# Holding back the first stores of a fused attention and channel-mix kernel, and moving its norms

## The chip, the cores and the metric

The kernel runs on one core of one Trainium2 chip. The metric is the device time of one execution in microseconds. Most executions of a kernel lie close together, but some are slower; a run more than 1.5% above the fastest of its kernel is called slow. Ratios are computed as the mean time of one kernel's fast runs over that of the other's fast runs of the same rounds, so they are not quite the ratio of the medians quoted beside them; the brackets are 95% intervals. A median is that of all runs, slow ones included; where that matters, the fast runs are named. The experiments ran on different chips (numbers 8, 11, 7, 15 and 2), so ratios compare kernels within one only.

## The reference

Two parts: cross-covariance attention over channels (256 x 256 per batch, 4 batches, 6208 rows), then an RWKV channel mix of the result.

```python
def _attn_ref(q, k, v, tau):
    qn = q / (np.linalg.norm(q, axis=1, keepdims=True) + 1e-06)
    kn = k / (np.linalg.norm(k, axis=1, keepdims=True) + 1e-06)
    s = kn.transpose(0, 2, 1) @ qn / tau
    s = s - s.max(-1, keepdims=True)
    a = np.exp(s)
    a /= a.sum(-1, keepdims=True) + 1e-09
    return (v @ a).astype(np.float32)

def _moe_ref(x, mu_k, mu_r, w_k, w_v, w_r):      # x_prev: x shifted by one row
    xk = mu_k * x + (1.0 - mu_k) * x_prev
    xr = mu_r * x + (1.0 - mu_r) * x_prev
    k = np.maximum(xk @ w_k, 0.0)
    v = k * k @ w_v
    r = 1.0 / (1.0 + np.exp(-(xr @ w_r)))
    return (r * v).astype(np.float32)
```

## The kernel before

After batch 0's q and k have been loaded and its softmax is done, the kernel walks through 48 blocks of 512 rows and a short last one. In the steps of block i it also multiplies q and k of the next batch (the "units"), loads v of block i + 6, transposes v of block i + 5 with a DMA, and computes x of block i + 2. SyncE issues both the v transposes and the stores of the results, in the order of the program (its ten issues from 64.13 to 118.33 us stand in that order in the profile of before):

```python
# in the steps of block i
if j == 0 and 4 <= i + 6 < NBLK - 1:
    v_load(i + 6)                    # GpSimd queue, 6 tiles
...
if j == 5 and 4 <= i + 5 < NBLK - 1:
    v_transpose(i + 5)               # SyncE queue, 5 tiles

def finish(i, s):                    # a quarter of block i's result; the last one in step 1 of block i + 1
    nc.scalar.activation(res[:, s], vr_ps[:, D:], AF.Tanh, scale=0.5)
    nc.vector.scalar_tensor_tensor(res[:, s], res[:, s], 1.0, vr_ps[:, :D], op0=OP.add, op1=OP.mult)
    ...
    if i < NBLK - 2:
        if s == S - 1:
            nc.sync.dma_start(dst, res)      # 512 KB, SyncE queue, res has 3 tiles
```

The sums of squares of batch 1 to 3 are added on VectorE; when the last add has been issued, the piece `norms` (four matmuls with one column, line L279) may be issued in the very next step:

```python
if len(chain) == NORMS and any(e[1] == holds[0] for e in adds):
    piece = None                     # norms wait for the last add
else:
    chain.pop(0)
```

Of the kernel before, what the change touches and what calls it, by code (L numbers as in the profile page):

```python
# [18 lines left out]
def kernel(  # L19
# [58 lines left out]
    bank = {}  # L78
    st_ps = {}
    adds = []  # L80
    sums = {}
    now = [0]
    groups = {}
# [29 lines left out]
    def group_load(b, g):  # L113
        rows, n = rows_of(b, g)
        if b == 0:
            t_f = []
            for i, t in enumerate((q, k)):
                f = pq.tile([P, S, C], F32, name=f"f{i}", tag=f"f{i}", bufs=6)
                (nc.sync if g else nc.scalar).dma_start(f[:rows, :n], qk_src(t, b, g))  # L119
                t_f.append(f)  # L120
            groups[b, g] = tuple(t_f)
        else:
            qk = pq.tile([P, S, 2, C], BF16, name="qk", tag="qk", bufs=5)
            groups[b, g] = (qk,)
            for i, t in enumerate((q, k)):
                nc.gpsimd.dma_start(rows_at(qk, b, g, i)[:rows, :n], qk_src(t, b, g))  # L126
# [79 lines left out]
    def unit_square(b, g, s):  # L206

        rows, n = rows_of(b, g)
        if s % 2:
            return  # L210
        qk = groups[b, g][0]
        if n == 1:
            t = sums[b, "left"] = pq.tile([P, 1, 2 * C], BF16, name="sq", tag="sq1", bufs=2)
            nc.scalar.activation(t[:rows], qk[:rows].rearrange("p s i c -> p s (i c)")[:, :1], AF.Square)
            return
        if s == 0:
            sums[b, g] = pq.tile([P, S, 2 * C], BF16, name="sq4", tag=f"f{g % 2}", bufs=6)
        t = sums[b, g]
        to = t[:, s:s + 2].rearrange("p s (i c) -> p i s c", i=2)
        if apart(b, g):  # L220
            nc.scalar.activation(to, qk.rearrange("p s i c -> p (s i c)").rearrange(
                "p (i s c) -> p i s c", i=2, s=S)[:, :, s:s + 2], AF.Square)
        else:
            nc.scalar.activation(t[:, s:s + 2], qk[:, s:s + 2].rearrange("p s i c -> p s (i c)"), AF.Square)  # L224
        if s == 2:
            adds.append((now[0] + 2, b, lambda: pairs_add(b, g)))
            adds.append((now[0] + 3, b, lambda: quad_add(b, g)))
# [38 lines left out]
    def softmax_pieces(b):  # L266

        s_ps = cov.pop(b) if b else None
        rn = pn.tile([P, 4], F32, name="rn")
        s_sb = pn.tile([P, 2, C], F32, name="s_sb")  # L270
        e_sb = pn.tile([P, 2, C], F32, name="e_sb", bufs=1)
        mx = pn.tile([P, 2], F32, name="mx")
        sm = pn.tile([P, 2], F32, name="sm")
        rk = rn[:, 2:4]
        def norms():
            bank[b] = ps.tile([P, 4], F32, name="bank", tag="xT_ps", bufs=2)
            t = sums.pop(b)
            for i in range(4):
                nc.tensor.matmul(bank[b][:, i:i + 1], t[:, i * P:(i + 1) * P], ones[:, 0:1],  # L279
                                 start=i == 0, stop=True, skip_group_check=True)  # L280

        def roots():
            nc.scalar.copy(rn, bank[b])

        def diagonals():
            dg = pn.tile([P, 2, P], F32, name="dg", tag="dg", bufs=1)
            for h in range(2):
                nc.vector.tensor_tensor(dg[:, h], cov[0][h][:, 3 * P * h:3 * P * h + P], ident_f, op=OP.mult)
            nc.vector.tensor_reduce(rn[:, 0:2], dg, axis=AX, op=OP.add)

        def root(h):
            nc.scalar.activation(rn[:, 2 * h:2 * h + 2], bank[0][:, 0:2] if h else rn[:, 0:2], AF.Sqrt)

        def invert_first(h):
            nc.vector.tensor_scalar_add(rn[:, 2 * h:2 * h + 2], rn[:, 2 * h:2 * h + 2], 1e-6)
            nc.vector.reciprocal(rn[:, 2 * h:2 * h + 2], rn[:, 2 * h:2 * h + 2])
            if h and inv_tau != 1.0:
                nc.vector.tensor_scalar_mul(rk, rk, inv_tau)

        def evac_first():  # L300
            for h in range(2):
                nc.vector.tensor_scalar_mul(s_sb[:, h], cov[0][h][:, P:P + C], rn[:, h:h + 1])

        def pow2():
            nc.gpsimd.tensor_tensor(rn, rn, half, op=OP.pow)

        def invert():
            nc.vector.tensor_scalar_add(rn, rn, 1e-6)
            nc.vector.reciprocal(rn, rn)
            for h in range(2):  # L310
                nc.vector.tensor_scalar_mul(s_sb[:, h], s_sb[:, h], rn[:, h:h + 1])
            if inv_tau != 1.0:
                nc.vector.tensor_scalar_mul(rk, rk, inv_tau)

        def evac():
            nc.scalar.copy(s_sb, s_ps)

        def turn():

            st_ps[b] = ps.tile([P, 2, C], F32, name="st_ps", tag="xT_ps", bufs=2)  # L320
            for n in range(4):
                ih, dh = divmod(n, 2) if b else (n % 2, n // 2)
                nc.tensor.transpose(st_ps[b][:, ih, dh * P:(dh + 1) * P], s_sb[:, dh, ih * P:(ih + 1) * P],  # L323
                                    ident_f)

        def exp(halves=range(2)):
            for ih in halves:
                if not bounded:
                    nc.vector.tensor_reduce(mx[:, ih:ih + 1], st_ps[b][:, ih], axis=AX, op=OP.max, negate=True)
                    nc.vector.tensor_tensor(mx[:, ih:ih + 1], mx[:, ih:ih + 1], rk[:, ih:ih + 1], op=OP.mult)  # L330
                nc.scalar.activation(e_sb[:, ih], st_ps[b][:, ih], AF.Exp, scale=rk[:, ih:ih + 1],
                                     bias=0.0 if bounded else mx[:, ih:ih + 1],
                                     accum_out=sm[:, ih:ih + 1])

        def shares():
            nc.vector.reciprocal(sm, sm)

        def weigh(ih):
            nc.scalar.activation(a_sb[:, b, ih, :], e_sb[:, ih], AF.Copy, scale=sm[:, ih:ih + 1])

        def weigh_first(ih):
            nc.vector.reciprocal(sm[:, ih:ih + 1], sm[:, ih:ih + 1])
            nc.vector.tensor_scalar_mul(a_sb[:, b, ih, :], e_sb[:, ih], sm[:, ih:ih + 1])

        if b == 0:
            return diagonals, root, invert_first, evac_first, turn, exp, weigh_first

        return [evac, None, norms, roots, pow2, None, invert, None, None, turn, lambda: exp([0]), lambda: exp([1]),
                shares, lambda: weigh(0), lambda: weigh(1)]

    blocks = [(b, t) for b in range(B) for t in range(NB)] + ["left"]
    NBLK = len(blocks)
    L1 = L + 1
    xl = const.tile([P, 2, B, L1], BF16, name="xl")
    st = {}

# [35 lines left out]

    def x_half(i, dh):
        b, t = blocks[i]
        if dh == 0:
            xT = p2.tile([P, 2, M + 1], BF16, name="xT", tag="xT", bufs=3)
            st[i, "x"] = xT
            if t == 0:
                nc.vector.memset(xT[:, :, 0:1], 0.0)
            else:  # L400
                nc.scalar.copy(xT[:, :, 0:1], st[i - 1, "x"][:, :, M:M + 1])
        xT = st[i, "x"]
        vT = st[i, "vT"]
        xT_ps = ps.tile([P, M], F32, name="xT_ps", tag="xT_ps", bufs=2)
        for ih in range(2):
            nc.tensor.matmul(xT_ps, a_sb[:, b, ih, dh * P:(dh + 1) * P], vT[:, :, ih, :],  # L406
                             start=ih == 0, stop=ih == 1)
        nc.scalar.copy(xT[:, dh, 1:], xT_ps)  # L408
# [120 lines left out]
    def down(i, j):  # L529
# [3 lines left out]
            return  # L533
        kk = st[i, "kk"]
        if j == 0:
            st[i, "res"] = p2.tile([P, S, D], F32, name="res", tag="res", bufs=3)
        if h == 0:
            vr_ps = ps.tile([P, 2 * D], F32, name="vr_ps", tag="vr_ps", bufs=2)
            st[i, "vr"] = vr_ps
# [9 lines left out]
    def finish(i, s):  # L549
# [8 lines left out]
        dst = out[b, t * M:(t + 1) * M, :].rearrange("(s p) c -> p s c", p=P)  # L558
        if i < NBLK - 2:
            if s == S - 1:  # L560
                nc.sync.dma_start(dst, res)
        elif s % 2:

            nc.sync.dma_start(dst[:, s - 1:s + 1], res[:, s - 1:s + 1])
# [1 line left out]
    def last_block(i):  # L566
# [1 line left out]
        down(i - 1, 7)  # L568
        kk, xr = st[i, "kk"], st[i, "xr"]
        SL = B * L // P  # L570
        res = p2.tile([P, S, D], F32, name="res", tag="res", bufs=3)
        r_ps = ps.tile([P, SL, D], F32, name="r_ps", tag="s_ps")
        y_ps = [ps.tile([P, D], F32, name="y_ps", tag="xT_ps", bufs=2) for _ in range(SL)]
        for s in range(SL):
# [71 lines left out]
    chain = []  # L646
    NORMS = 13
    holds = [0]

    def unit(ahead=2):  # L650

# [57 lines left out]
    for i in range(-2, NBLK - 1):  # L709
        for j in range(8):  # L710
# [6 lines left out]
                v_load(i + 6)  # L717
            if chain:
                piece = chain[0]
                if len(chain) == NORMS and any(e[1] == holds[0] for e in adds):  # L720
                    piece = None
                else:
                    chain.pop(0)
# [53 lines left out]
                unit()  # L777
            if adds and adds[0][0] <= now[0] and (j in (1, 6, 7) or adds[0][1] == holds[0] and chain):
                next_add()
            now[0] += 1  # L780
            if i >= 0 and i % NB == 2 and j == 1 and i // NB < B:
                left_go[0] = left_x(i // NB)
# [40 lines left out]
```

## Time and profile before

| | before |
|---|---|
| timed runs | 506.85, 506.85, 508.45 us |
| profiled execution | 515.58 us, span 513.8 us, slow |
| instructions | 9206 |

The top of the page (busy us, share of the span, count) and, from its fourth part, the chain that ended last by engine:

```profile
PE 480.6 (94%) x3370; PEld 330.9 (64%) x3429; DVE 431.4 (84%) x788; ACT 428.6 (83%) x869; POOL 96.4 (19%) x143
...
PE 73%; DMA 21%; DVE 2%; issue 1%; POOL 1%; ACT 1%; SPq 0%; POOLq 0%; DVEq 0%
```

PE is busy nearly always, yet a fifth of the chain is DMA: there is a stretch in which PE runs behind transfers.

### The profile page before, as it was taken

The numbers are of one execution on the slowest core, as the hardware profiler recorded it, in microseconds if no ns is written. First come the engines' busy times: TensorE is split into PE (matmuls) and PEld (weight loads), VectorE is DVE, ScalarE is ACT, GpSimd is POOL, SyncE is SP. The second block draws the span as 40 slices with busy tenths as digits, with TensorE's granted clock in tenths as the row PEclk, the third lists the DMA queues.
The fourth block names the chain that finished last, engine by engine and source line by source line (L and its number), as shares of the span: only waits on it lengthen the run. The fifth ranks groups of instructions, "written<-read, shape, count | busy, mean of one in ns | idle before, by whom it ended". The sixth has DMA issues, their size and how long they took to land.

```text
span 513.8 us, 9206 instructions
## 1 busy us (share of the span) xinstructions
PE 480.6 (94%) x3370; PEld 330.9 (64%) x3429; DVE 431.4 (84%) x788; ACT 428.6 (83%) x869; POOL 96.4 (19%) x143
## 2 busy tenths in 40 slices
PE   3579999797899999999999999999999999999996
PEld 1345677555676677677676667667666666666675
DVE  3778799957979989989988988989988787878884
ACT  5769997877889989898899989898888888878884
POOL 0043331222143132221143132200031100000000
PEclk9999999989999999999999999999999999999999
DMA  8999999999999999999799999974299673523123
GB/s 325 409 307 197 191 165 134 173 145 209 164 213 174 211 172 179 179 160 168 113 158 149 221 161 188 181 134 111 63 150 161 102 146 83 106 74 93 41 84 103
DMA packets 132694, 83.46 MB, mean 162 GB/s; under 512 B 50660, under 2 KB 125736, under 8 KB 132648
## 3 DMA queue, kind: packets, MB, share of 16 engines
q0 software_dynamic: 55824, 33.01, 50.4%
q1 hardware_dynamic: 76504, 49.59, 43.5%
q8 instruction: 27, 0.44, 0.4%
q10 hardware_dynamic: 320, 0.26, 0.2%
q14 instruction: 19, 0.16, 0.1%
HBM read 78.71 MB, written 25.43 MB: 203 GB/s over the span
## 4 chain that ended last, share of the span: by engine, by line
PE 73%; DMA 21%; DVE 2%; issue 1%; POOL 1%; ACT 1%; SPq 0%; POOLq 0%; DVEq 0%
PE vr_ps L546 28%; PE kT_ps L514 25%; DMA vT<-v_bf 11%; PE vr_ps L542 8%; PE xT_ps L406 7%; DMA f<-in_q_dram 5%; PE s_ps L263 4%; DMA v_bf<-in_v_dram 2%; DMA qk<-in_q_dram 2%; DMA qk<-in_k_dram 1%; POOL v_bf L363 0%; DVE kk L527 0%; SPq L119 0%; PE y_ps L584 0%; PE st_ps L323 0%
## 5 line engine op out<-in xcount | busy, mean ns | idle before, releaser
L519 ACT ACTIVATE kr<-kT_ps 128x512 bf16<-128x512 f32 (+1 forms) x390 | 235.0, 605 | 34.2 <-PE kT_ps L514 28.6
L546 PE MATMUL vr_ps<-w_v_sb,kk 128*128 128x256 bf16 x1536 | 230.6, 273 | 0.4
L514 PE MATMUL kT_ps<-xk,w_k_sb 128*128 128x512 bf16 (+1 forms) x722 | 218.1, 377 | 0.3 <-DVE xk L499 0.2
L546 PEld LDWEIGHTS <-kk 128*128 128x128 bf16 x1536 | 150.4, 98 | 57.5
L556 DVE SCALAR_TENSOR_TENSOR res<-res,vr_ps 128x256 f32<-128x256 f32 x192 | 80.0, 417 | 59.9 <-ACT res L555 59.9
L527 DVE TENSOR_TENSOR kk<-kr 128x2048 bf16<-128x2048 bf16 (+1 forms) x148 | 125.8, 851 | 0.2 <-ACT kr L519 0.2
L514 PEld LDWEIGHTS <-w_k_sb 128*128 128x128 bf16 x780 | 75.7, 98 | 28.0 <-issue 1.4
L555 ACT ACTIVATE res<-vr_ps 128x256 f32<-128x256 f32 x192 | 76.8, 400 | 2.3 <-PE vr_ps L546 1.3
L408 ACT CAST xT<-xT_ps 128x512 bf16<-128x512 f32 x94 | 55.9, 594 | 26.8 <-PE xT_ps L406 26.4
L542 PE MATMUL vr_ps<-w_r_sb,xr 128*128 128x256 bf16 x384 | 73.5, 273 | 2.7
L499 DVE SCALAR_TENSOR_TENSOR xk<-delta,mu_t,xT 128x512 bf16<-128x512 bf16 x94 | 70.1, 746 | 0.0
L499 DVE SCALAR_TENSOR_TENSOR xr<-delta,mu_t,xT 128x512 bf16<-128x512 bf16 x94 | 70.0, 746 | 0.0
L542 PEld LDWEIGHTS <-xr 128*128 128x128 bf16 x384 | 37.7, 98 | 45.3 <-issue 1.5
L406 PE MATMUL xT_ps<-vT,a_sb 128*128 128x512 bf16 x188 | 56.3, 381 | 6.2 <-DMA vT<-v_bf 6.2
L263 PE MATMUL s_ps<-qk 128*128 128x256 bf16 (+1 forms) x294 | 56.0, 273 | 0.0
L126 POOL DMA_DIRECT2D qk<-in_q_dram x39 | 26.1, 670 | 152.7 <-ACT kr L519 128.8
L224 ACT ACTIVATE sq<-qk 128x1024 bf16<-128x1024 bf16 x48 | 51.1, 1064 | 0.0
L363 POOL DMA_DIRECT2D v_bf<-in_v_dram x48 | 36.6, 765 | 56.3 <-DMA vT<-v_bf 35.2
L189 PE MATMUL s_ps<-qk 128*128 128x384 bf16 (+2 forms) x98 | 19.2, 339 | 17.1 <-ACT qk L146 15.2
L489 DVE TENSOR_TENSOR delta<-xT 128x1024 bf16<-128x1024 bf16 x47 | 32.2, 686 | 1.1 <-ACT xT L408 1.1
L263 PEld LDWEIGHTS <-qk 128*128 128x128 bf16 (+1 forms) x294 | 28.6, 98 | 5.7 <-issue 0.8
L126 POOL DMA_DIRECT2D qk<-in_k_dram x39 | 25.8, 662 | 19.8 <-DMA v_bf<-in_v_dram 11.2
(106 smaller groups left out, 249.8 us busy)
## 6 DMA issues: line engine op xcount, KB each, us to landing
out_dram<-res SPq DMA_DIRECT2D x47, 512.0 KB, 5.0
v_bf<-in_v_dram POOLq DMA_DIRECT2D x48, 256.0 KB, 8.1
qk<-in_q_dram POOLq DMA_DIRECT2D x36, 256.0 KB, 7.2
qk<-in_k_dram POOLq DMA_DIRECT2D x36, 256.0 KB, 8.9
f<-in_q_dram SPq DMA_DIRECT2D x11, 512.0 KB, 9.5
f<-in_k_dram SPq DMA_DIRECT2D x11, 512.0 KB, 10.0
vT<-v_bf SPq DMA_TRANSPOSE x44, 7.8
f<-in_q_dram SPq DMA_DIRECT2D x2, 256.0 KB, 9.0
```

The lines of the kernel that those rows point to most:

```text
L126: nc.gpsimd.dma_start(rows_at(qk, b, g, i)[:rows, :n], qk_src(t, b, g))
L263: nc.tensor.matmul(s_ps[:, ih, :], rows_at(qk, b, g, 0)[:rows, s, ih * P:(ih + 1) * P], rows_at(qk, b, g, 1)[:rows, s, :], start=t0 and ih ...
L406: nc.tensor.matmul(xT_ps, a_sb[:, b, ih, dh * P:(dh + 1) * P], vT[:, :, ih, :], start=ih == 0, stop=ih == 1)
L408: nc.scalar.copy(xT[:, dh, 1:], xT_ps)
L499: nc.vector.scalar_tensor_tensor(o[:, dh], st[i, "d"][:, dh], mu[:, dh:dh + 1], st[i, "x"][:, dh, :M], op0=OP.mult, op1=OP.add)
L514: nc.tensor.matmul(kT_ps[:, :m], w_k_sb[:, dh, fh * P:(fh + 1) * P], xk[:, dh, :m], start=dh == 0, stop=dh == 1)
L519: nc.scalar.activation(kr, kT_ps[:, :m], AF.Relu, scale=0.5 ** 0.5)
L527: nc.vector.tensor_tensor(st[i, "kk"][:, fh // 4 * 4 + lo:fh + 1, :m], kr, kr, op=OP.mult)
L542: nc.tensor.matmul(vr_ps[:, D:], xr[:, dh, s * P:(s + 1) * P], w_r_sb[:, dh, :], start=dh == 0, stop=dh == 1)
L546: nc.tensor.matmul(vr_ps[:, :D], kk[:, fh, s * P:(s + 1) * P], w_v_sb[:, fh, :], start=fh == 0, stop=fh == 7)
L555: nc.scalar.activation(res[:, s], vr_ps[:, D:], AF.Tanh, scale=0.5)
L556: nc.vector.scalar_tensor_tensor(res[:, s], res[:, s], 1.0, vr_ps[:, :D], op0=OP.add, op1=OP.mult)
```

## The change

The intent is to take the stores of the first blocks out of a stretch in which loads, transposes and stores crowd the DMA engines (DMA share 1.15 to 1.59 in the stretches of 12 us from 60 to 132 us of the profile of before), and to let the norms of batch 1 not wait for their sum. The results need tiles while they are held; they take those of batch 0's q loads, eight of them now, and the square sums keep to the other six.

```diff
-                f = pq.tile([P, S, C], F32, name=f"f{i}", tag=f"f{i}", bufs=6)
+                f = pq.tile([P, S, C], F32, name=f"f{i}", tag=f"f{i}", bufs=8 - 2 * i)
...
-            sums[b, g] = pq.tile([P, S, 2 * C], BF16, name="sq4", tag=f"f{g % 2}", bufs=6)
+            sums[b, g] = pq.tile([P, S, 2 * C], BF16, name="sq4", tag="f1", bufs=6)
...
+    HOLD = 6
+    stores = []
...
-            st[i, "res"] = p2.tile([P, S, D], F32, name="res", tag="res", bufs=3)
+            st[i, "res"] = pq.tile([P, S, D], F32, name="res", tag="f0", bufs=8)
...
             if s == S - 1:
-                nc.sync.dma_start(dst, res)
+                stores.append((dst, res))
+                while len(stores) > max(0, HOLD - max(0, i - NB // 2)):
+                    nc.sync.dma_start(*stores.pop(0))
...
-                if len(chain) == NORMS and any(e[1] == holds[0] for e in adds):
+                if len(chain) == NORMS and (any(e[1] == holds[0] for e in adds) or now[0] < added[0] + 3):
                     piece = None
...
                 next_add()
+                added[0] = now[0]
```

(Left out: the same tile for the last block's result, the start value `added = [0]`, and an assertion on the order of the softmax pieces.)

More of the change, by code (lines that the diff above doesn't have):

```diff
@@ L80 @@
     adds = []
+    ready = set()
     sums = {}
@@ L338, in weigh @@
         def weigh(ih):
+            ready.add((b, ih))
             nc.scalar.activation(a_sb[:, b, ih, :], e_sb[:, ih], AF.Copy, scale=sm[:, ih:ih + 1])
@@ L394, in x_half @@
         b, t = blocks[i]
+        assert b == 0 or {(b, 0), (b, 1)} <= ready
         if dh == 0:
@@ L570, in last_block @@
         SL = B * L // P
-        res = p2.tile([P, S, D], F32, name="res", tag="res", bufs=3)
+        res = pq.tile([P, S, D], F32, name="res", tag="f0", bufs=8)
         r_ps = ps.tile([P, SL, D], F32, name="r_ps", tag="s_ps")
@@ L648 @@
     holds = [0]
+    added = [0]
     def unit(ahead=2):
```

## The prediction

> **What bounds the kernel now.** I read the page's busy table, then busy time by stretch, then what PE waited for, then the SyncE queue in order of time, then the chain that ended last. PE is busy 480.6 of 513.8 us (94%), so what matters is where the other 33 us lie. Busy time by stretch tells (columns: us, busy time and instruction count of PE, PEld, DVE, ACT, POOL, granted clock, DMA share, GB/s):
>
> ```profile
> 84.00:96.00 12.00, 11.81 (x85) 8.19 (x85) 10.69 (x20) 9.95 (x20) 3.39 (x6) 1.00 1.25 181
> 96.00:108.00 12.00, 9.24 (x54) 5.84 (x55) 8.36 (x15) 7.70 (x16) 2.55 (x4) 0.86 1.37 183
> 108.00:120.00 12.00, 8.46 (x60) 5.95 (x61) 7.85 (x14) 7.28 (x16) 3.69 (x5) 1.00 1.15 155
> ...
> 132.00:144.00 12.00, 10.45 (x79) 7.27 (x79) 9.66 (x17) 9.46 (x22) 1.48 (x2) 1.00 1.48 178
> 144.00:240.00 96.00, 95.31 (x672) 66.64 (x683) 87.17 (x156) 86.38 (x177) 27.98 (x38) 1.00 1.22 179
> 240.00:372.00 132.00, 131.05 (x934) 92.08 (x951) 118.94 (x212) 117.85 (x243) 25.40 (x34) 1.00 0.93 150
> ```
>
> From 144 us on PE is busy 99.3% of the time: there nothing but fewer matmuls helps. Up to 36 us the kernel loads batch 0, which the change leaves as it is. Between, PE loses 2.76 us in 96 to 108, 3.54 us in 108 to 120 and 1.55 us in 132 to 144. What PE waited for names them (waiter, what it waited for, us in total, times, longest):
>
> ```profile
> PE xT_ps L406 <- DMA vT<-v_bf: 6.2, 2, 3.4
> PE bank L279 <- DVE sq L247: 1.4, 1, 1.4
> ```
>
> Two waits for a transposed v tile, one for the last sum of squares of batch 1. Why the tiles are late stands in the SyncE queue, in order of time (start, us, instruction):
>
> ```profile
> 64.13 0.68 SPq L561 DMA_DIRECT2D out_dram<-res  x1
> 65.00 10.85 SPq L371 DMA_TRANSPOSE vT<-v_bf  x1
> 75.94 0.67 SPq L561 DMA_DIRECT2D out_dram<-res  x1
> 76.77 13.17 SPq L371 DMA_TRANSPOSE vT<-v_bf  x1
> 90.03 0.53 SPq L561 DMA_DIRECT2D out_dram<-res  x1
> 90.67 15.21 SPq L371 DMA_TRANSPOSE vT<-v_bf  x1
> 105.98 0.53 SPq L561 DMA_DIRECT2D out_dram<-res  x1
> 106.61 3.38 SPq L466 DMA_TRANSPOSE vlT<-vl_bf  x1
> 110.08 8.15 SPq L371 DMA_TRANSPOSE vT<-v_bf  x1
> 118.33 0.53 SPq L561 DMA_DIRECT2D out_dram<-res  x1
> ```
>
> The queue has no gap from 64 to 118 us: 50.8 of these 54 us (10.85 + 13.17 + 15.21 + 3.38 + 8.15) go to pushing transposes, each right behind a 512 KB store. The same instruction takes 2 to 5 us after 144 us. The 8.15 one ends at 118.23, and the starved x product starts at 118.26. The chain that ended last agrees: one piece of it is two transposes, 41.45 us from 76.77.
>
> [...]in 60 to 72 us the software queue took 79.6% and the hardware queue 42.8% of the engines' packet time, at only 176 GB/s. [...]SyncE waited 248.5 us in all for results of L556 ahead of stores. [...]Here the first wait (2.7 us) was followed by a granted clock of 0.86 in its stretch and an x product of 1.01 us for two matmuls against 0.59; after the 3.4 us wait it was 0.59[...].
>
> **The change part by part.** No instruction is added or removed on PE, DVE, ACT or POOL that costs anything; the instruction orders differ on PE, DVE and ACT only round the norms of batch 1, and on SyncE.
>
> Part 1, stores. The code lets store 0 go at the end of block 6, then two per block until block 12. Six stores of 512 KB, 3.1 MB, leave the stretch 64 to 126 us. The stretches of 12 us from 60 to 132 moved 2.11 + 1.22 + 2.17 + 2.20 + 1.87 + 2.43 = 12.0 MB, so a quarter of the bytes goes. The order of SyncE shows a second effect that the diff doesn't tell: now eight v transposes and the small one come in a row before the first store. Before, the transpose of block n + 6 stood behind the store of block n, which waits for block n to finish, so it could start some three blocks before its use. Now it waits only for its v load and a free tile of the five: some five blocks. Two block pitches of 9.5 us are 19 us more lead, against lateness of 2.7 and 3.4 us. I expect both waits to go: 6.2 us, and the slow clock: 54 matmuls took 9.24 us in 96 to 108, and at the usual 0.139 us (11.81 over 85) would take 7.5, so 1.7 us. In the profiled execution this is 7.9 us.
>
> Part 2, norms. They move about one step (18 PE rows) later. The wait of 1.4 us ends at 141.39 when the sum lands; one step of other matmuls takes about 1.2 us, so I count 1.2 us gained. The pieces behind shift as well; the last one, weighing a_sb, ended at 157.84, about 159 then, and its first reader on PE comes at about 159.7. It just fits.
>
> Part 3, results in batch 0's eight load tiles, and the square sums in six tiles. Those loads are read by 36 us, so nothing waits there. A result tile comes round after eight blocks; store 0 must land before block 8 writes. SyncE gets to it early, since it no longer waits for results, so that seems safe. Before, three tiles cost ACT one wait of 1.0 us.
>
> Sum for a profiled execution: 7.9 + 1.2 = 9.1 us of 515.6.
>
> But the timed runs give 506.85 (one 508.45) and the profiled one 515.58, marked slow: 8.7 us apart. Of those none can lie after 144 us, where matmuls are back to back at the full granted clock, and the load phase runs at 319 to 410 GB/s[...]. 515.58 - 7.9 = 507.7, nearly the timed value: recording seems to slow the DMA, and the transpose waits seem to be mostly an effect of the profiled execution. This is an inference, not a reading. So I give the timed runs 1.2 us for the norms and about 1.1 us, a seventh of the 7.9, for what is left of the other: 506.85 - 2.3 = about 504.5 us.
>
> **The rivals.** (A) The timed runs have the transpose waits in full: gain 9.1, time 497.7. For it: the chain runs over them. Against it: 8.7 us would need another home. (B) The stores come back in blocks 6 to 12, two per block, so 1.0 MB of stores and 256 KB of transposes per 9.5 us, some 135 GB/s on the hardware queue, where it moved 1.36 MB in 12 us (113 GB/s) at most so far. DMA packet share is 1.2 to 1.5 there already. Then transposes of blocks 12 to 18 are late, or q and k, or block 8 waits for a tile: 508 to 512. Against it: a lead of five blocks is used up slowly in six blocks, and from block 8 on q and k come in at four units per block, not six. (C) The loads on the software queue slow the transposes, not the stores: the profile keeps most of the 6.2 us; the timed runs get the norms alone: 505.6. For it: 79.6% against 42.8%. (D) PE takes the norms' wait elsewhere, as DVE is busy without a gap from 133 to 142: 506.5.
>
> **Range and chances.** I give 0.6 to timed runs without transpose waits (505.6), 0.3 to a third or half of them there (502.3) and 0.1 to A (497.5): mean 503.8, median near 505. I predict 504.5, with 499.5 to 507.2 for eight in ten. 2% is 10.1 us, below 496.7, more than all that the profile offers: faster 0.04; slower needs 517: 0.02; same 0.94.
>
> **What would show it right or wrong.** Right: the waits for vT gone from PE's list, PE above 11.8 in every stretch of 12 us from 60 on, clock 1.00 in 96 to 108, SyncE running transposes in a row well under 10 us each, the wait of L279 under 0.3 us, and profiled and timed runs within 2 us of each other. Wrong: a wait for vT after block 12 (from 150 us on), ACT waiting for the result store in block 8, q and k late in 120 to 190 us (rival B), transposes still above 10 us with no store beside them (C), or a timed gain above 6 us, which would mean that the waits were there in timed runs too (A).

6.2 us of waits and 1.7 us of slow clock are 7.9, with 1.2 us for the norms 9.1 in a profiled execution; for timed runs 1.2 + 1.1 = 2.3, and 506.85 - 2.3 gives about 504.5 us. That the slow clock would go with the waits was the estimate; the trace shows only that it came at the end of the first wait (granted clock 0.50 for 3.41 us, from 102.7 us on, the wait ending at 103.00). The transposes after 144 us took 1.25 to 5.25 us in the trace.

## The result

506.34 us median of four runs (505.64 to 506.94) against 506.88 us (506.85 to 508.45), ratio 0.9981 [0.9958, 1.0004]. The time is within 2% of the kernel before and inside the range that was forecast; the gain between the medians is 0.5 us, where 2.3 us were forecast.

The same two views of the page after, busy time and chain:

```profile
PE 480.2 (95%) x3370; PEld 331.8 (66%) x3429; DVE 431.3 (85%) x788; ACT 428.9 (85%) x869; POOL 96.9 (19%) x143
...
PE 86%; DMA 7%; DVE 4%; issue 1%; ACT 1%; SPq 0%; POOL 0%; DVEq 0%; POOLq 0%
```

The DMA share of the chain fell from 21% to 7%, and the span of the profiled execution from 513.8 to 505.2 us. Busy time by stretch of the changed kernel (columns as in the prediction):

```profile
36.00:48.00 12.00, 10.78 (x84) 7.48 (x84) 8.15 (x25) 8.36 (x22) 6.84 (x11) 0.86 1.18 189
...
84.00:96.00 12.00, 11.95 (x87) 8.39 (x86) 11.16 (x21) 11.13 (x23) 2.86 (x5) 1.00 1.30 163
96.00:108.00 12.00, 11.89 (x88) 8.62 (x89) 11.25 (x20) 11.13 (x23) 3.28 (x5) 1.00 1.32 116
108.00:120.00 12.00, 11.89 (x90) 8.51 (x90) 11.68 (x22) 11.13 (x23) 4.08 (x6) 1.00 1.48 146
...
132.00:144.00 12.00, 11.86 (x89) 8.43 (x90) 11.90 (x24) 10.70 (x23) 5.97 (x7) 1.00 1.25 256
```

PE is full in every stretch from 60 us on (11.86 to 11.95 of 12 us up to 144 us), and the list of what PE waited for is empty there: both waits for vT and the wait of the norms are gone. One stretch is worse than before: in 36 to 48 us the granted clock is 0.86 (1.00 in the profile of before), of which more below. The SyncE queue in order of time:

```profile
54.26 30.47 SPq L375 DMA_TRANSPOSE vT<-v_bf  x5
84.83 1.22 SPq L471 DMA_TRANSPOSE vlT<-vl_bf  x1
87.98 21.49 SPq L375 DMA_TRANSPOSE vT<-v_bf  x3
109.53 0.58 SPq L568 DMA_DIRECT2D out_dram<-res  x1
117.10 1.54 SPq L375 DMA_TRANSPOSE vT<-v_bf  x1
118.69 2.33 SPq L568 DMA_DIRECT2D out_dram<-res  x2
```

Eight v transposes go out before the first store, 30.47 us for five and 21.49 for three, so 6 to 7 us each, waits included, where the four v transposes of 65 to 118 us took 8 to 15 before. So the profiled executions differ by 8.6 us, and the timed runs say 0.5. The question is where the rest is.

### The profile page after: what moved, and what is told of

The parts are those of the page before. It is cut to its first block, busy times and chain, and to the rows that moved or that the text cites. A ratio compares the mean times of both kernels' runs of the same rounds, so it can differ in the third digit from the quotient of the medians.

```text
span 505.2 us, 9205 instructions
## 1 busy us (share of the span) xinstructions
PE 480.2 (95%) x3370; PEld 331.8 (66%) x3429; DVE 431.3 (85%) x788; ACT 428.9 (85%) x869; POOL 96.9 (19%) x143
## 4 chain that ended last, share of the span: by engine, by line
PE 86%; DMA 7%; DVE 4%; issue 1%; ACT 1%; SPq 0%; POOL 0%; DVEq 0%; POOLq 0%
PE vr_ps L551 32%; PE kT_ps L519 29%; PE vr_ps L547 10%; PE xT_ps L411 8%; PE s_ps L264 6%; DMA f<-in_q_dram 6%; DMA v_bf<-in_v_dram 1%; DVE kk L532 1%; DVE xk L504 1%; DVE res L561 1%; PE st_ps L324 0%; PE x_ps L435 0%; DVE xr L504 0%; PE vT_ps L384 0%; DVE delta L494 0%
## 5 line engine op out<-in xcount | busy, mean ns | idle before, releaser
L190 PE MATMUL s_ps<-qk 128*128 128x384 bf16 (+2 forms) x98 | 19.7, 346 | 16.5 <-ACT qk L147 15.1
## 6 DMA issues: line engine op xcount, KB each, us to landing
out_dram<-res SPq DMA_DIRECT2D x47, 512.0 KB, 5.1
f<-in_q_dram SPq DMA_DIRECT2D x11, 512.0 KB, 9.6
f<-in_k_dram SPq DMA_DIRECT2D x11, 512.0 KB, 10.0
```

## The experiments

A quantity that recurs is the **lead of block 7**: from the landing of its v transpose (its issue on SyncE plus the time to landing that the trace gives) to its first x product on PE. In the profile of before it was 0.0 us, since PE stood waiting for it; in that of the changed kernel it was 12.5 us. Block 8, whose first x product ended the second wait of before, is named beside it where it says more. Where `prof` gives no time to landing, the last update of the transpose's semaphore in the packed trace was taken.

### Controls and the two halves

Two runs repeat the kernels, two do one half of the change each.

Before again (no edit):

> The kernel before, unchanged, as a control. Theory 1: the transpose waits of the first profile (6.2 us of waiting, 1.7 us of slow clock after it) belong to a rare slow execution, and most executions have none; then this profile, if it falls in a fast execution, shows under 1 us of waits for vT, and a span of 504 to 506 us, and its ratio to the kernel before is 1.000 within 0.002. Theory 2: the waits are in every execution and the changed kernel gives their gain back elsewhere; then this profile again shows about 6 us of waits for vT, and the timed runs still 506.9.

Changed again (no edit):

> The changed kernel again, for a tighter ratio and a second profile. Theory 1: 0.997 to 0.999 (0.5 to 1.5 us), all runs fast, no PE wait after 60 us. Theory 2: the same ratio, but a PE, ACT or DVE wait after 60 us that the kernel before has not. The slow clock from 38.7 to 42.1 us of its first profile should come and go from run to run and cost 1.2 us where it comes.

The stores alone: the change with this line put back:

```diff
-                if len(chain) == NORMS and (any(e[1] == holds[0] for e in adds) or now[0] < added[0] + 3):
+                if len(chain) == NORMS and (any(e[1] == holds[0] for e in adds)):
```

> The stores held and the tiles changed, the norms as before. Theory 1: no waits for vT, the wait of the norms (1.4 us in the profile of before) still there, so 0.999 to 1.001 in the timed runs. If the norms' wait came only from the late loads of a slow execution, it is gone here as well, and the ratio is that of the whole change. Theory 2: nothing gained, some wait after block 6.

The norms alone: the kernel before with

```diff
+    added = [0]
...
-                if len(chain) == NORMS and any(e[1] == holds[0] for e in adds):
+                if len(chain) == NORMS and (any(e[1] == holds[0] for e in adds) or now[0] < added[0] + 3):
...
                 next_add()
+                added[0] = now[0]
```

> The norms three steps behind alone, the stores as before. Theory 1: the whole of the timed gain is here, 0.997 to 0.999, and a slow execution may still show the waits for vT. If the norms' wait was an effect of the slow execution: 1.000.

Measured, all on one chip in the same rounds, with 11 runs of the kernel before beside them (507.07 to 509.03, median 507.7):

| | six runs, us | median | ratio |
|---|---|---|---|
| before again | 507.01, 508.24, 508.75, 509.81, 517.52, 520.76 | 509.28 | 1.0012 [0.9991, 1.0032] |
| changed | 505.47, 505.55, 505.60, 505.63, 505.64, 507.32 | 505.62 | 0.9961 [0.9946, 0.9976] |
| stores alone | 506.62, 506.88, 506.95, 507.05, 508.18, 509.10 | 507.00 | 0.9992 [0.9975, 1.0010] |
| norms alone | 505.50, 505.84, 506.71, 506.86, 509.55, 509.95 | 506.78 | 0.9993 [0.9963, 1.0023] |

What PE waited for in the second profile of the kernel before, in 60 to 130 us and in 130 to 200 us:

```profile
PE xT_ps L406 <- DMA vT<-v_bf: 1.2, 1, 1.2
...
PE bank L279 <- DVE sq L247: 1.4, 1, 1.4
```

and of the stores alone, in 130 to 200 us:

```profile
PE bank L280 <- DVE sq L248: 1.4, 1, 1.4
```

Three things follow. First, the wait for vT is not a constant of the kernel: 6.2 us in one execution, 1.2 in another, and 0 in the norms alone, whose transposes stand behind the stores as before (lead of block 7: 0.0, 2.0 and 2.6 us). The wait of 1.2 us was for block 8: its transpose landed at 112.45 us and its x product began at 112.49, and in the norms alone too it landed only 0.04 us before its product, by the trace's semaphore updates. Second, the norms' wait of 1.4 us is there whenever the norms are not moved, to the tenth of a microsecond, and gone when they are. It shows in the lowest runs: 507.01 and 507.07 for the kernel before and 506.62 for the stores alone, against 505.50 for the norms alone and 505.47 for both. Third, slow executions (517.52, 520.76) also occur in timed runs of the kernel before, so they are not peculiar to the executions whose profile was kept, and the one of the changed kernel whose profile was kept took 505.60 us, among the 505.47 to 507.32 of its others. The changed kernel gains 2.1 us here between the medians, not 0.5.

The first comparison was small partly because of the clock of 36 to 48 us. The changed kernel's first PE products in that stretch, in order of time, in its first profile:

```profile
38.71 1.11 PE L324 MATMUL st_ps<-ident_f,s_sb 128*128 128x128 f32 x4
...
45.13 0.59 PE L411 MATMUL xT_ps<-vT,a_sb 128*128 128x512 bf16 x2
```

and in the profile of its third run, below:

```profile
38.18 0.66 PE L324 MATMUL st_ps<-ident_f,s_sb 128*128 128x128 f32 x4
...
43.67 0.59 PE L411 MATMUL xT_ps<-vT,a_sb 128*128 128x512 bf16 x2
```

The same four transposes take 1.11 us at the low clock (0.50 for 3.41 us in the packed trace of the first profile) and 0.66 at the full one. From their start to the first regular x product it is 6.42 us (45.13 - 38.71) against 5.49 (43.67 - 38.18), so 0.9 us, and the start is 0.5 us later as well. Five of the 20 profiles (changed, before again, stores alone, norms alone twice) have 0.86 there, the others 1.00. Two of the four runs of the first comparison have a mean clock of 0.997 (506.94 and 506.47), and all four of the changed kernel's runs above 507 us have 0.993 to 0.997, while its runs at 0.998 to 1.000 lie between 505.27 and 506.20. That is the mean clock of a whole run: that it was lost in 36 to 48 us is seen only in the profiles. Nor is it peculiar to the changed kernel, as the other four profiles with 0.86 show.

### The place in the queue or the bytes

The held stores change two things at once: the transposes no longer stand behind stores in SyncE's queue, and the bytes of the stores leave the crowded stretch.

Queue alone: the kernel before, with the first six stores issued from ScalarE:

```diff
-            if s == S - 1:
+            if s == S - 1 and i < HOLD:      # HOLD = 6
+                stores[i] = (dst, res)
+            elif s == S - 1:
                 nc.sync.dma_start(dst, res)
...
+            if j == 4 and i - 1 in stores:
+                nc.scalar.dma_start(*stores.pop(i - 1))
```

> The kernel before, but the stores of blocks 0 to 5 go out at their old time from the ScalarE queue, three steps later, so that no transpose stands behind them in the SyncE queue, while all their bytes still move in the same stretch. So far block 7's transpose lands 0.0 to 2.6 us ahead of its first x product with the early stores and 5 to 12.5 us ahead with the held ones. If the place in the queue is what counts, the lead of block 7 is above 5 us here; if it is the bytes[...], it stays under 3 us. Timed runs: the norms' wait is still in, so 0.999 to 1.002; ACT pays six issues of about 0.5 us, which it may or may not hide.

Bytes alone: the changed kernel, with 16 KB of each result stored at the old place (blocks 0 to 11):

```diff
-                stores.append((dst, res))
+                if i < 2 * HOLD:
+                    nc.sync.dma_start(dst[:16, s], res[:16, s])
+                    stores.append(((dst[:, :s], res[:, :s]), (dst[16:, s], res[16:, s])))
...
```

> The changed kernel, but 16 KB of every block's result goes out at the old time and at the old place of the queue, so that the transposes stand behind the results as in the kernel before, while 97% of the bytes are held. If the bytes count, the lead of block 7 is above 5 us here as well, and the time is the changed kernel's, 0.995 to 0.998; if the place in the queue counts, the lead falls to 0 to 3 us and waits for vT may come back.

Measured: lead of block 7 of 7.0 us for the queue alone and of 11.4 us for the bytes alone. Each half by itself lifts it over the 0.0 to 4.5 us that the five profiles with early stores behind SyncE show (before 0.0, before again 2.0, norms alone 2.6, 3.6 and 4.5), into the range of the profiles with held stores (5.0 to 12.5). For block 8 it is 7.1 and 12.4 us, against 0.0 to 1.3 and 6.6 to 13.1. So the sharp question had the answer "either". With one profile each, the two sizes can't be told apart.

One explanation of the queue's share can be ruled out for this stretch: that a store whose result is not ready holds the transpose behind it. What SyncE waited for before stores, in 55 to 126 us, in the profile of before and in the bytes alone:

```profile
SPq L561 <- DVE res L556: 0.9, 2, 0.5
SPq L561 <- DVE kk L527: 0.4, 1, 0.4
...
SPq L567 <- DVE res L561: 22.8, 3, 8.2
SPq L567 <- DVE sq L236: 22.1, 3, 8.6
```

The kernel before waited 1.3 us there; its SyncE was busy issuing transposes (50.8 of the 54 us from 64 to 118). The bytes alone waited some 45 us for VectorE before its stores, and still has a lead of 11.4 us. In time, the queue alone (six issues on ScalarE, 0.38 to 0.41 us each in its profile) took 508.67 us median (506.65 to 510.54), ratio 1.0024 [0.9997, 1.0050], and the bytes alone 507.17 (505.99 to 507.53), ratio 0.9982 [0.9964, 1.0000]. The first has the norms' wait and the second does not, so 1.4 us of the distance may be the norms'.

### Does the tail go away?

A third run of the changed kernel (no edit):

> The changed kernel a third time. The kernel before had three executions above 515 us in about twenty, the changed one none in ten. If the held stores take this tail away, all six runs stay under 508 us and the ratio is 0.995 to 0.998. One run above 510 us would speak against it.

Measured: 505.27 to 507.44, median 505.5, ratio 0.9960 [0.9941, 0.9979], as expected; the kernel before had one run of 515.15 among its 11. A later pair ran the changed kernel and the norms alone in the same rounds (no edits):

> The changed kernel, in the same rounds as the norms alone. If the held stores are worth something in ordinary executions, its mean is 0.5 to 1.5 us below that of the norms alone; if they only guard against rare slow ones, the medians agree within 0.5 us and only the norms alone has runs above 508.5.

> The norms alone, in the same rounds as the changed kernel: 506.3 to 507.0 median, lowest 505.5; with a tail above 508.5 if the held stores matter.

Measured: changed 505.44, 505.68, 506.01, 506.04, 507.34 and 512.29, median 506.03, ratio 0.9981 [0.9937, 1.0025]; norms alone 505.67, 506.41, 507.40, 508.49, 510.23 and 514.04, median 507.95, ratio 1.0001 [0.9966, 1.0036]. The kernel before had 506.99 to 516.94, median 508.53. So one run of the changed kernel is above 508.5 after all: the held stores do not exclude such executions. The fast runs' means are 507.1 and 507.6 us, 0.5 us apart with overlapping intervals, so this pair does not decide between the two readings that were expected. And the norms alone, once more:

> The norms alone once more. Its first six runs had 505.5 and 505.84 as the changed kernel has, but also 509.55 and 509.95. If the held stores are worth something in timed runs, it is in such runs: again one or more of six above 508.5, the lowest at 505.5. If not, all six lie within 505.3 to 507.5 as the changed kernel's do.

Measured: 505.74 to 507.31, median 506.68, ratio 0.9956 [0.9919, 0.9993], with no run above 508.5. The expectation of a tail failed here and held in the pair. Over all, 1 of 22 runs of the changed kernel is above 508.5 us (median 505.64), 4 of 18 of the norms alone (median 506.96) and 24 of 61 of the kernel before (median 508.06). These counts mix chips, so they only suggest: about 1 us for the norms and about 1 us for the stores.

### Keeping PE's clock up

Could the changed kernel be helped by idle matmuls in the load phase?

```diff
         cov_first(g, diagonals)
+        if NB - 4 <= g < LAST:
+            keep_warm(3)
...
+    keep_warm(2)
     go = v_transpose_pe(0, nc.vector.tensor_copy)
```

> The changed kernel with three idle matmuls after each of the last groups of batch 0 and two before the first transposes of v, where PE waits for ACT or DMA anyway. In three of five profiles the granted clock was 0.86 in 36 to 48 us, and x products and transposes ran at half speed for about 3.5 us, which cost 1.2 to 1.3 us. If PE's idleness in the load phase causes it, it is gone here: clock 1.00 in 36 to 48 us, all runs within 0.3 us of 505.6, ratio 0.994 to 0.996. If the matmuls get in the way of the load phase, the first x product of block 0 comes later than 41.3 us.

Measured: clock 1.00, five of six runs 506.60 to 506.90, but one of 512.0; median 506.66, ratio 0.9995 [0.9961, 1.0029]. The first x product of block 0 came at 41.45 us instead of 40.24: the matmuls after groups 11 and 12 met no idle time. So they were put only where PE waits:

```diff
         cov_first(g, diagonals)
+        if 4 < g < DIRECT:
+            keep_warm(3)
```

> The changed kernel with three idle matmuls (0.64 us) after groups 5 to 10 of batch 0 alone, where PE then still waits 0.45 us for ACT, and none where PE does not wait: in the run before, those after groups 11 and 12 and before the transposes of v put the first x product off by 1.2 us and ate the gain. If the idleness of the load phase causes the slow clock in 36 to 48 us: clock 1.00 in every execution, all runs 505.2 to 505.8, ratio 0.995 to 0.9965, against 5 of 6 runs at 505.5 in the third run of the changed kernel. If its phase is chance: one to three of six runs still at 506.5 to 507.5.

Measured: 505.9, 506.62, 506.69, 506.87, 507.16, 512.1; median 506.78, ratio 0.9977 [0.9933, 1.0022]. The profiled run had the clock at 1.00, but the others were not at 505.5, so this is no better than the changed kernel. Four of these other runs have a mean clock of 0.998 to 1.000 and still took 506.6 to 507.2 us, so a full clock alone does not bring 505.5. No version beats the changed kernel.

### Taking lead away

Four tiles for loaded v instead of six, in the kernel before and in the changed one, were meant to take lead away in every execution:

```diff
-        v_bf = p2.tile([P, S, C], BF16, name="v_bf", tag="v_bf", bufs=6)
+        v_bf = p2.tile([P, S, C], BF16, name="v_bf", tag="v_bf", bufs=4)
```

> The kernel before with four tiles for loaded v rows instead of six, to take away lead in every execution, not only in the slow ones. Loads of blocks 11 to 13 then wait for the transposes of blocks 7 to 9, which land 0 to 3 us ahead of use. If the margin of those transposes is what decides, PE waits 2 to 12 us for vT in the profile and the ratio is 1.004 to 1.025. If the margin does not matter: 1.000 and no such wait.

> The changed kernel with four tiles for loaded v rows. Its transposes of blocks 7 to 9 land 5 to 13 us ahead of use, so the loads of blocks 11 to 13 are put off little. If the margin decides: under 2 us of waits for vT, ratio to the kernel before 0.995 to 1.000, so that the gap between changed and unchanged grows from 2 us to 4 us or more. If held stores give nothing but the norms: it loses as much as the kernel before with four tiles.

Measured: before with four tiles 511.17 to 511.43, ratio 1.0052 [1.0011, 1.0093]; changed with four tiles 509.80 to 510.11, ratio 1.0024 [0.9984, 1.0065]. The first ratio lies in the range expected, but not from waits for vT, and the second does not. There is no wait for vT in either; the lead of block 7 even rose, to 6.8 and 20.1 us. Two stretches of the kernel before with four tiles:

```profile
48.00:60.00 12.00, 11.83 (x92) 8.14 (x91) 10.17 (x17) 11.83 (x22) 1.34 (x3) 1.00 0.98 157
60.00:72.00 12.00, 9.43 (x61) 5.72 (x59) 6.66 (x13) 7.97 (x17) 7.75 (x14) 1.00 1.13 179
```

The load of block 6's v waited for its tile until 58.7 us (46.0 before), and the loads of q and k behind it in GpSimd's queue with it, so PE starved once in 60 to 72 us, behind ScalarE, which waited 3.3 us for a load of k. But the DMA engines were less crowded in 48 to 60 us (share 0.98, where the kernel before has 1.29), and the transposes of blocks 4 and 5 landed 3.3 and 3.1 us after their issue instead of 12.5 and 17.6. No store goes out before 64 us in either profile: in 48 to 60 us the software queue took 127.9% of the engines' packet time in the kernel before and 74.5% here, so here the slow transposes came with more loads. It was an accident of this experiment, but the clearest run on that point. It is also the steadiest kernel: four runs within 0.3 us in both versions. Between the two versions lie 1.5 us (511.40 and 509.93), and the norms' wait of 1.4 us is in the first alone: where neither waits for vT, nothing is seen of a gain by the held stores.

Then extra loads of q that nobody reads, 256 KB each, ten of them from ScalarE in blocks 0 to 4, on the norms alone and on the changed kernel:

```diff
+            if j in (2, 6) and 0 <= i < 5:
+                extra = pq.tile([P, S, C], F32, name="extra", tag="extra", bufs=1)
+                nc.scalar.dma_start(extra[:, :2], qk_src(q, 0, 1 + i)[:, :2])
```

> The norms alone, with ten extra loads of 256 KB that nobody reads, from the ScalarE queue during blocks 0 to 4, to load the DMA engines more in every execution. Its transposes of blocks 7 to 9 land only 1.4 to 3.6 us ahead of use without them. If that lead is what decides: waits for vT of 4 to 20 us in the profile, 510 to 526 us. If not: under 1 us of waits, 506 to 508 us[...].

> The changed kernel with the same ten extra loads. Its transposes land 5 to 12.5 us ahead without them. If the lead decides, it swallows most of the extra traffic: waits for vT at most a third of those of the norms alone with extra loads, and at least 4 us faster than it. If the held stores are worth nothing, both lose the same.

Measured: 532.35 us median (521.2 to 538.9) and 522.43 (517.24 to 532.61), most of them slow; the fast runs are one of 521.2 against 517.24 and 517.63. The difference looks like support, but neither profile has a wait for vT. What ScalarE waited for in the first, 60 to 120 us:

```profile
ACT kr L519 <- DMA extra<-in_q_dram: 10.2, 2, 5.3
```

The loads shared one tile, and each waited on ScalarE for the one before: the test was spoiled. It was repeated with eight tiles of 256 KB (`tag="extra", bufs=8`):

> The norms alone, with the ten extra loads of 256 KB in eight tiles. ScalarE should wait for none of them. If the lead decides: waits of PE for vT of 4 to 20 us in the profile, 510 to 525 us. If not: under 1 us of waits for vT, 506 to 508 us.

> The changed kernel with the same extra loads in eight tiles. If the lead decides: at least 3 us faster than the norms alone with them, and waits for vT at most half of its. If the held stores are worth nothing in time: both within 1 us of each other.

Measured: norms alone 513.04, 513.84, 518.42, 518.56; changed 515.78, 517.36, 520.97 and two slow runs, 526.46 and 529.81. The ratios of the fast runs are 1.0153 [1.0086, 1.0220] and 1.0165 [1.0099, 1.0231], so there was no 3 us advantage. In the norms alone PE waited as foreseen, and the lead of block 7 was 0.0:

```profile
PE xT_ps L406 <- DMA vT<-v_bf: 4.9, 2, 2.7
```

In the changed kernel PE waited for no vT, but ScalarE did, before it issued an extra load, and PE behind ScalarE. The first line is PE's wait, the second ScalarE's:

```profile
PE kT_ps L519 <- ACT kr L524: 13.4, 3, 5.0
```

```profile
ACT kr L524 <- DMA vT<-v_bf: 20.1, 3, 7.2
```

The packed trace tells why: each of the three loads that were held waits for the semaphore that it is itself to raise, and a transpose had been given the same one; the first went out at 80.07 us, when block 5's transpose had landed at 80.05. So the wait stands in the program: the extra loads brought a wait that the test was to be free of. The wait of PE in the norms alone fits the first half of the theory, that more traffic turns a small lead into waits, but the first profile of before has as long a wait without the extra loads. The second half, that held stores save time under such traffic, is left without a valid test.

## Why the prediction was right or wrong

**The mechanism of the stores held in its direction.** The waits for vT were gone, PE was above 11.8 in every stretch from 60 us on, transposes took 6 to 7 us each in a row, and none of the signs named for rival B came: no wait for vT after block 12, none of ScalarE for the results' tiles, q and k not late. Rival C is half right: in one profile each, stores alone, queue place alone and fewer loads give lead.

**The size of the lead was wrong.** Forecast were 19 us more. The median lead of block 7 is 2.6 us over the five profiles with early stores and 9.2 us over the seven with held ones and no other change to the transfers, so some 7 us more. For blocks 8 to 12 the same medians grow by 8 to 15 us, still short of 19. The step that failed is "some five blocks": in the changed kernel's first profile the transposes of blocks 7 to 12 were issued 32 to 36 us before their first x product, which is 3.2 to 3.6 blocks of 10 us, against 18 to 28 us in that of before. "Now it waits only for its v load and a free tile" was right, but the v loads themselves land late: the transposes of blocks 8, 9 and 10 were issued 0.1 to 0.7 us after their v had landed (at 79.3, 88.0 and 95.3 us).

**Another step of the mechanism failed too:** that the transpose of block n + 6 "stood behind the store of block n, which waits for block n to finish". The 248.5 us that the prediction quotes for it are those of the whole run; in 55 to 126 us they are 0.9 us. The prediction's own lines show SyncE issuing transposes there without a gap. So unready results did not delay the transposes there; by one profile each, the stores' bytes and their place did.

**One reading was a coincidence.** The prediction took the transpose that ended its issue at 118.23 us for the one that PE waited for until 118.26. It was the transpose before it, issued at 90.67. The chain of waits of the kernel before has them as one piece (start, us, what):

```profile
76.77 41.45 DMA vT<-v_bf x2
```

Two flights, about 26 us (76.77 to 103.0, where the first wait ends) and about 15 us more to 118.2: block 7's and block 8's. They landed 12 to 13 us after SyncE was done with issuing them. The argument for holding the stores survives, but the issue time on SyncE was a poor measure of the delay.

**The norms were nearly exact.** Forecast 1.2 us, seen 1.4 us, in all five profiles without the move (before twice, stores alone, queue alone, before with four tiles) and in none with it. The last softmax piece fitted, as forecast: no wait of PE for a_sb after block 0.

**The step that failed in the sum is the last one**, from the profiled execution to the timed runs: "recording seems to slow the DMA", hence 506.85 minus 2.3. The experiments speak against the first half: executions above 515 us come among the timed runs too, the waits for vT were 6.2, 1.2 and 0 us in three profiles with early stores, and the first profile of before fell in a slow execution. The consequence drawn from it, that most timed runs lack most of the wait, seems right, for the wrong reason, so the forecast of 1.2 + 1.1 us was not far off: 2.1, 1.9 and 2.5 us between the medians in the three later calls with the changed kernel, against 0.5 in the first. The other term that failed is the base. It took 506.85 us, two of three early runs, for the kernel's time; that is close to the lowest of 61 runs (506.62), whose median is 508.06. And the sum had no term for the clock in 36 to 48 us, which seems to cost the changed kernel's runs about 1 to 2 us in about one run in four and met two of its first four.

In the terms of the sum, for the first comparison: the 1.2 us of the norms are there between the lowest runs (506.85 and 505.64); the 1.1 us for waits left in timed runs had little to come from, since three of the four runs of before lay at 506.85 to 506.91, near the lowest of all; and the slow clock took some back. This split is read off eight runs and is not proved.

**The rivals.** A (waits in full in every timed run, 497.7 us) fell: no run came near. D (the norms' wait taken elsewhere) fell with the norms' profile.

**What stays open.** How much of the gain in time is the held stores': the ratio of the stores alone is 0.9992 [0.9975, 1.0010], and the changed kernel and the norms alone have overlapping intervals. What the slow executions of the kernel before are made of was seen in one profile only (6.2 us of waits for vT). No profile was kept of the changed kernel's run of 512.29 us.

## What to carry to other kernels

When a profile is slower than the timed runs, profile the unchanged kernel again before explaining the difference: here, where the transposes landed 0 to 4.5 us ahead of need, the wait for them was 6.2, 1.2 and 0 us in three profiles, and the lead of the transfer told more than the wait. A total of waits over the whole run says nothing of one stretch: ask for the waits of the stretch itself, as with the 248.5 us here of which 0.9 us counted. To forecast a gain of 2 us, first know the spread of the kernel before; three runs of one chip gave a base that was 1.2 us below the median of 61.

## What the traces show of transposes and of the granted clock

- In a quieter stretch, that of the kernel before with four tiles, 48 to 60 us (DMA share 0.98), 256 KB transposes landed 3.2 us after their issue and a 256 KB load of v 3.8 us after its own. In a crowded one, the profile of before, 74 to 90 us (DMA share 1.52), two transposes took 24.5 us and loads of 256 KB 15.1 to 18.5, and the transpose issued next, at 90.67 us, held SyncE for 15.21 us.
- In 5 of 20 profiles the granted clock fell to 0.86 in 36 to 48 us, though in the changed kernel's first profile PE's longest wait in 12 to 48 us was 1.2 us. In the first profile of before, a wait of 2.7 us was followed by two matmuls of an x product in 1.01 us, but one of 3.4 us by 0.59 and full speed. So the length of one wait does not tell. Just before the low clock of the changed kernel, in 36.4 to 38.6 us, PE ran matmuls of one column and transposes; the third run of the changed kernel had them too and kept its clock (1.00). What sets it was not found.
